# An adaLN block with sliding-window attention and a token-mixing MLP: V's outer rows copied from PSUM, two units' products moved ahead of their dense groups, the last quotients ahead of the last norm, the first group reordered

## The chip, the cores and the metric

One core of one Trainium2 chip runs the whole program. The metric is the device time of one execution in microseconds (us); the time before the change is the median of three runs. Engines are named as the profile names them: PE (TensorE matmuls), PEld (its weight loads), DVE (VectorE), ACT (ScalarE), POOL (GpSimd), SP (SyncE, which issues the DMAs here). Each engine works through its own instructions in order and waits on semaphores for the others.

## The reference, cut to what matters

```python
# x: 2048 x 512, 32 heads of 16, window of 256
h = _layernorm(x) * (1 + ca) + sa              # sa, ca, ga, sb, cb, gb = silu(c) @ w_mod
q, k, v = split(h @ wqkv)
p = softmax(where(0 <= i - j < 256, q @ k.T / 4, -1e9))
x = x + ga * ((p @ v) @ wo)
h = _layernorm(x) * (1 + cb) + sb
u = gelu(einsum('bsd,sf->bdf', _layernorm(h), w1) + b1)     # mixes the 2048 tokens, F = 1792
x = x + gb * transpose(einsum('bdf,fs->bds', u, w2) + b2)
```

## The kernel before

**Groups and units.** The 2048 tokens are worked in four groups `tg` of 512. In a group the 32 heads are taken eight at a time (`g8`), and eight heads make up to five units `k` (`KINDS`, L413): k = 0 and 1 are the inner keys of the even heads, k = 2 the outer rows of both parities (keys that share a 64-row half with their queries' block), k = 3 and 4 the inner keys of the odd heads. In the first group k = 0 and 3 are one unit for g8 > 0. This makes 77 units. Each has scores on PE (`emit_scores`), two exponentials of 128x1024 on ACT (`emit_exp`, L676) and products with V on PE (`av_a` L696 with `VaugT`, `av_c` L715 with `Vc`), which add up in the one PSUM bank `po`. V carries 16 columns of ones behind each head's 16 columns, so the row sums come out beside the products.

**PSUM.** The scores use three buffers of two banks (`pss`), the products one bank (`po`), and everything dense one bank (`dn`): a dense group must wait until DVE has evacuated the dense group before it.

**What else runs beside the attention.** One dense group is laid beside almost every unit by `plan` (L857): q, k and v projections of this group and the next (`qk_group`, `v_group`), the transposes of the normalised x, the output projection `wo_group`, and parts of the first MLP product (`part_group`, which need the blocks `hb`). Most dense groups are 16 matmuls and one evacuation on DVE.

**The order inside a unit u** (L1003 to L1061) is on PE: scores of unit u + 1, then the products of unit u - 1 if they close a sum (`closes`, L1026), then the dense group, then the products of unit u - 1 if they close nothing. The exponential of the first half is emitted ahead of all this and that of the second half behind the dense group.

**DVE and POOL** get the rest from `fill` (L818): a list of chains whose steps are taken when a hand-kept clock says that they fit before the next evacuation (`SLACK` 0.3 us plus `late[0]`). Chains are the statistics of the first norm, `norm_rest` (L753: reciprocal `zr` on DVE, the quotients `merge` on POOL at L760, a transpose `OTd` back on DVE at L768) and `ln23` (L771) for each of the first twelve token blocks: p1 statistics of the new x (DVE) and its reciprocal root (POOL, L208 and L212), p2 the norm on DVE (L788) and two passes over 128x512 on POOL (L792, L793), p3 statistics of the result (DVE) and `hb` on POOL (L219). p2 is free to start when fewer than `LIVE` = 4 blocks are under way.

**V's outer rows.** `v_group`'s evacuation (L303) copies PSUM to `VaugT` (L304), and for the third and fourth block of a group copies the first 64 rows of heads 0 to 7, values and ones, from there to `Vc` (L306). The other rows of `Vc` come by DMA (`copy_vc`).

**The start** (L547 to L577, L994 to L1035): the first group's q and k for the first eight heads come in pieces (`first_qk`), the four parts of the second k piece ahead of unit 0's scores; block 3 of V is computed at unit 1, behind the scores of unit 2.

**The end** (L1062 on): after the last products come `norm_rest` of the last eight heads, then `t_wo` (L1130), whose matmuls need `OTd`, among the first matmuls of the MLP's first product (L1111), the rest of it (L1197), and the second product (L1233).

Of the kernel before, what the change touches and what calls it, by code (L numbers as in the profile page):

```python
# [30 lines left out]
def kernel(  # L31
# [261 lines left out]
    def v_group(tg, tl, pool, name="dn"):  # L293
        def mms(parts=range(ND), pv=None):
            pv = pv or pool.tile([P, D], DT.float32, name=name)
            for dc in parts:
                dense(
                    pv, lhsT=h1T[tg][:, dc, tl * P : (tl + 1) * P],
                    rhs=wqkv[:, dc, 2 * D : 3 * D], start=(dc == 0), stop=(dc == ND - 1),
                )  # L300
            return pv

        def evac(pv):  # L303
            nc.vector.tensor_copy(out=VaugT[tg][:, tl, :, 0:DH], in_=pv[:].rearrange("p (h d) -> p h d", d=DH))  # L304
            if tl > 1:
                nc.vector.tensor_copy(out=Vc[0][0:64, tl, 0:8, :], in_=VaugT[tg][0:64, tl, 0:8, :])  # L306
        return mms, evac, 0.9 if tl > 1 else 0.7

    q_loads = []
# [59 lines left out]
    def bias_group(pool):  # L369
        def mms():  # L370
            pb = pool.tile([P, NF + NT], DT.bfloat16, name="dn")
            nc.tensor.transpose(pb[:], b12[:], identity[0 : NF + NT, 0 : NF + NT])
            return pb

        def evac(pb):
            nc.vector.tensor_copy(out=bFM[:], in_=pb[:])
        return mms, evac, 0.2
# [37 lines left out]
    with tc.manual_schedule():  # L415
# [98 lines left out]
        def ones(r):  # L514
            for b in range(4):
                nc.gpsimd.memset(Vring[r][:, b, :, DH : 2 * DH], 1.0)

        ones(0)

        def zeros_for(g8):  # L520
            for half in range(2):
# [51 lines left out]
            first_qk("k", dc, 0)  # L573
        q_half(0)
        k_piece(0)
        for dc in range(ND):
            first_qk("k", dc, 1)  # L577

        w1box = {}
# [191 lines left out]
        def ln23(tb):  # L771
            v = {}

            def stats(src, key):
                st = small.tile([P, nc.vector.BN_STATS_DIM], DT.float32, name="ln2_stats")
                nc.vector.bn_stats(out=st[:], in_=src)  # L776
                v[key] = small.tile([P, nc.vector.BN_AGGR_DIM], DT.float32, name="ln2_mv")
                nc.vector.bn_aggr(out=v[key][:], in_=st[:])  # L778
                v[key + "r"] = rstd_of(v[key][:, 1:2], 1, "ln2")

            def p1():
                stats(xres[tb][:], "m2")
                return 0.85

            def p2():
                live.add(tb)
                h2 = v["h2"] = lnpool.tile([P, D], DT.bfloat16, name="h2")
                nc.vector.tensor_scalar(  # L788
                    out=h2[:], in0=xres[tb][:], scalar1=v["m2"][:, 0:1], scalar2=v["m2r"][:],
                    op0=ALU.subtract, op1=ALU.mult,  # L790
                )
                nc.gpsimd.tensor_tensor(out=h2[:], in0=h2[:], in1=bc_cb1, op=ALU.mult)  # L792
                nc.gpsimd.tensor_tensor(out=h2[:], in0=h2[:], in1=bc_sb, op=ALU.add)  # L793
                return 2.4

            def p3():
                stats(v["h2"][:], "m3")
                apply_by_pool(hb[tb][:], v["h2"][:], v["m3"][:, 0:1], v["m3r"][:])
                done.add(tb)
                live.discard(tb)  # L800
                return 2.0
            return [(p1, 0.8), (p2, 0.37, lambda: len(live) < LIVE), (p3, 0.8)]

        chains = []
        live = set()
        loaded = set(range(8))
        clock = dict(pe=0.0, act=0.0, dve=0.0, pool=0.0, dn=0.0, po=0.0)

        held, late = [False], [0.0]

        def add_chain(steps, first=False):
            chains.insert(0 if first else len(chains), [list(steps), clock["dve"]])
# [44 lines left out]
        def plan(tg):  # L857
            at, then = {}, {}

            def lay(ul, group):  # L860
                assert ul not in at, (tg, ul)
                at[ul] = group

            def qk(ul, g, g8, kind):
                lay(ul, qk_group(g, g8, kind, ps_dn))

            if tg == 0:
                lay(0, v_group(tg, 1, ps_po, "po"))
                lay(2, qk_group(tg, 1, "k", ps_po, "po"))
                lay(3, v_group(tg, 2, ps_dn))  # L870
                for ul, g8, kind in ((1, 1, "q"), (4, 2, "q"), (5, 2, "k"), (6, 3, "q"), (7, 3, "k")):
                    qk(ul, tg, g8, kind)
                lay(8, bias_group(ps_dn))
                lay(9, bc_group(ps_dn))
                then[12] = [(lambda g=g: fold_wod(g), 0.0) for g in range(ND)]
            else:
                lay(0, v_group(tg, 2, ps_dn))
                lay(1, v_group(tg, 3, ps_dn))
                if tg == 1:
                    order = ((2, 1, "k"), (3, 2, "q"), (4, 2, "k"), (5, 3, "q"), (8, 3, "k"))  # L880
                else:
                    order = ((2, 2, "k"), (3, 3, "q"), (4, 3, "k"))
                for ul, g8, kind in order:
                    qk(ul, tg, g8, kind)
                for ul, fc, k in {2: ((8, 10, 0), (10, 11, 0)), 3: ((8, 13, 0), (10, 12, 0), (11, 12, 1))}.get(tg, ()):
                    lay(ul, part_group(fc, k))
                for ul in (6, 7, 9, 10) if tg == 1 else (5, 6, 7, 9):
                    tb = next(wo_next)
                    lay(ul, wo_group(tb, ps_dn))
                    then[ul] = ln23(tb)  # L890
            if tg + 1 < NG:
                t0, t1, q0, v0, k0, q1, v1 = (10, 11, 12, 14, 13, 16, 15) if tg == 0 else (11, 12, 13, 14, 15, 17, 16)
                lay(t0, transpose_group(tg + 1, 0, ps_dn))
                lay(t1, transpose_group(tg + 1, 1, ps_dn))
                lay(v0, v_group(tg + 1, 0, ps_dn))
                lay(v1, v_group(tg + 1, 1, ps_dn))
                for ul, g8, kind in ((q0, 0, "q"), (k0, 0, "k"), (q1, 1, "q")):
                    qk(ul, tg + 1, g8, kind)
                if tg:
                    qk(18, tg + 1, 1, "k")  # L900
                    qk(19, tg + 1, 2, "q")
            else:
                for n, fc in enumerate((6, 7, 8, 9)):
                    for k in range(2):
                        lay(12 + 2 * n + k, part_group(fc, k))
            return at, then
# [85 lines left out]
                on_pool(for_pool)  # L992

        emit_scores(0)  # L994
        for dc in range(ND):
            first_qk("q", dc, 1)
        q_half(1)
# [5 lines left out]
        for u, (tg, g8, k) in enumerate(units):  # L1003
# [19 lines left out]
                av_c(tg, g8, 1)  # L1023
            for n in range(3) if u == 4 else ():
                products(n)
            closes = u > 0 and units[u - 1][2] in (2, 4) and u != 3  # L1026
            if closes:
                products(u - 1)
            if u == 1:
                mms, evac, cost = v_group(0, 3, ps_s)  # L1030
                pv = mms(range(ND), ps_s.tile([P, 2, 4 * P], DT.float32, name="pss")[:, 0, :])
                clock["pe"] += 0.9
                evac(pv)
                ln1_stats(1, 1)
                clock["dve"] = max(clock["dve"], clock["pe"] + 0.05) + cost + 0.8  # L1035
            group = at.get(ul)
            held[0] = u < 4

            late[0] = 0.5 if 4 <= u < 8 else 0.12 if tg else 0.0
            if group:  # L1040
                tile_ = group[0]()
                clock["pe"] = max(clock["pe"], clock["dn"]) + (0.55 if group[2] > 1 else 0.2 if group[2] == 0.2 else 0.9)
# [2 lines left out]
            if group:  # L1045
                fill(clock["pe"] + 0.05)
                evacuate(group, tile_)
                if u == 1:
                    on_pool(1.0)
                    for tl in range(2):  # L1050
                        ln1_apply(1, tl)
                    on_pool(2.26)
                if ul in then:
                    add_chain(then[ul])
            if u > 3 and not closes:
                products(u - 1)
            if both(tg, g8, 0) and k == 4:
# [4 lines left out]
        u += 1  # L1062
        emit_av(u - 1)
        add_chain(norm_rest(NG - 1, ND - 1), first=True)
        while chains:
            clock["dve"] += 1.0
            fill(clock["dve"] + 9.0)
# [202 lines left out]
```

## Time and profile before

| what | value |
|---|---|
| three runs | 259.0, 257.82, 258.76 us; median 258.76 |
| the profiled execution's own time | 259.11 us |
| its span (first to last instruction) | 257.2 us |
| granted PE clock | 1.0 throughout |
| busy: PE, DVE, ACT, POOL | 239.2, 171.3, 159.3, 132.6 us |
| the exponentials (L676) | 154, busy 142.7 us, first at 12.8, last at 160.7 |
| the MLP's second product (L1233) | 238 matmuls, 48.5 us |

Times in views are counted from the span's start. A timeline row gives the start, the time that the merged instructions took, engine, line, operation, what it writes and reads, the count, and in brackets the idle time of the engine ahead of it with what ended it. A row "line engine op ... xcount | busy, mean ns | idle" groups all instructions of one line. A row of windows gives the busy time of each engine, with the count of its instructions, in one stretch of time.

### The profile page before, as it was taken

What the parts mean: (1) busy time and instruction counts of PE and PEld (TensorE: products, weight loads), DVE (VectorE), ACT (ScalarE), POOL (GpSimd) and SP (SyncE); (2) the same over time, 40 slices, a digit from 0 to 9 for tenths busy, and PEclk for the clock granted to TensorE, in tenths of its full rate; (3) what the DMA queues carried; (4) which work ended last, traced back from release to release, by engine and by line L of the source; (5) the groups of instructions that cost most, each with busy time, mean ns of one, the idle gap of its engine ahead of it and who ended that gap; (6) DMA issues with size and microseconds to landing.
All of it is one profiled execution on the core that took longest, in us unless ns stands there. A gap on an engine that the chain in (4) does not pass through costs nothing.

```text
span 257.2 us, 11303 instructions
## 1 busy us (share of the span) xinstructions
PE 239.2 (93%) x5011; PEld 127.3 (49%) x5011; DVE 171.3 (67%) x358; ACT 159.3 (62%) x187; POOL 132.6 (52%) x225
## 2 busy tenths in 40 slices
PE   7999889999899889999989999889999999999994
PEld 2644455555455455565555555444444444444443
DVE  5758789887887797887887888589603212332544
ACT  6388999999899899999999999100065220000000
POOL 5697876886468688568666499955300000000000
PEclk9999999999999999999999999999999999999999
DMA  5986715157422623201122200999930000202021
GB/s 176 324 260 199 218 59 144 36 144 195 130 66 70 171 49 66 56 4 34 31 60 57 55 3 14 331 414 409 412 144 0 0 0 3 82 0 82 33 92 41
DMA packets 26260, 29.96 MB, mean 116 GB/s; under 512 B 3940, under 2 KB 22884, under 8 KB 26212
## 3 DMA queue, kind: packets, MB, share of 16 engines
q1 hardware_dynamic: 26212, 29.25, 36.5%
q8 instruction: 39, 0.64, 1.0%
q14 instruction: 9, 0.07, 0.1%
HBM read 22.55 MB, written 2.23 MB: 96 GB/s over the span
## 4 chain that ended last, share of the span: by engine, by line
PE 62%; DVE 19%; POOL 12%; issue 3%; DMA 2%; SPq 1%; POOLq 0%
PE py L1233 19%; PE dn L288 14%; PE pu L1111 7%; PE pu L1197 6%; PE pss L609 4%; DVE t L748 3%; PE po L715 3%; PE po L696 3%; DVE VaugT L304 3%; POOL ln_rstd L212 2%; DMA wmod<-in_w_mod_dram 2%; POOL h L793 2%; POOL h L792 2%; DVE ln_stats L776 2%; POOL merge L760 2%
## 5 line engine op out<-in xcount | busy, mean ns | idle before, releaser
L676 ACT ACTIVATE et<-pss 128x1024 bf16<-128x1024 f32 (+1 forms) x154 | 142.7, 1025 | 6.5 <-PE pss L626 4.9
L1233 PE MATMUL py<-guT,w2r 128*128 128x512 bf16 (+1 forms) x238 | 48.5, 367 | 0.0
L1233 PEld LDWEIGHTS <-w2r 128*128 128x128 bf16 x238 | 23.3, 98 | 25.3
L288 PE MATMUL dn<-h1T,wqkv 128*32 128x512 bf16 (+1 forms) x480 | 31.4, 378 | 2.4 <-DVE VaugT L304 1.4
L1212 DVE SCALAR_TENSOR_TENSOR o<-py,bFM,bc 128x512 bf16<-128x512 f32 (+1 forms) x17 | 11.7, 714 | 30.5 <-PE py L1233 30.5
L748 DVE STREAM_TRANSPOSE t<-po 128x512 f32<-128x512 f32 x32 | 22.9, 714 | 6.9 <-PE po L715 4.3
L212 POOL TENSOR_TENSOR ln_rstd<-ln_ve,mhalf 128x1 f32<-128x1 f32 (+1 forms) x40 | 24.1, 603 | 3.4
L609 PE MATMUL pss<-QT,KT 32*128 32x64 bf16 (+2 forms) x704 | 25.4, 237 | 0.0
L696 PE MATMUL po<-et,VaugT 128*32 128x64 bf16 (+2 forms) x704 | 24.7, 240 | 0.7 <-DVE t L748 0.7
L696 PEld LDWEIGHTS <-VaugT 128*32 128x32 bf16 x704 | 18.1, 96 | 12.0 <-issue 4.2
L208 POOL TENSOR_SCALAR ln_ve<-ln_mv 128x1 f32<-128x1 f32 (+1 forms) x39 | 9.2, 235 | 24.6 <-DVE ln_mv L778 12.9
L609 PEld LDWEIGHTS <-KT 32*128 32x128 bf16 x704 | 13.9, 92 | 12.4 <-issue 3.8
L288 PEld LDWEIGHTS <-wqkv 128*32 128x32 bf16 x544 | 14.0, 95 | 11.7 <-issue 4.1
L792 POOL TENSOR_TENSOR h<-h,bc 128x512 bf16<-128x512 bf16 x12 | 13.9, 1161 | 8.7 <-DVE h L788 8.7
L1122 ACT ACT_TABLE_LOAD x1 | 1.3, 1283 | 27.0 <-issue 27.0
L760 POOL TENSOR_TENSOR merge<-t,zr 128x512 bf16<-128x512 f32 x16 | 17.0, 1060 | 0.9 <-DVE zr L759 0.9
L288 PE MATMUL dn<-wqkv,h1T 128*32 128x512 bf16 x224 | 15.0, 380 | 2.3 <-DVE VaugT L304 0.9
L626 PE MATMUL pss<-mask_q,mask_k 32*128 32x256 bf16 (+1 forms) x232 | 16.7, 266 | 0.0
L1120 DVE TENSOR_TENSOR gelu_a<-pu,part 128x512 f32<-128x512 f32 x8 | 5.2, 686 | 16.4 <-PE pu L1197 16.4
L288 PE MATMUL dn<-hb,w1a 128*32 128x512 bf16 x208 | 13.8, 380 | 0.9 <-DVE part L851 0.7
L793 POOL TENSOR_TENSOR h<-h,bc 128x512 bf16<-128x512 bf16 x12 | 13.9, 1158 | 0.9
L1197 PE MATMUL pu<-hb,w1b 128*128 128x512 bf16 x64 | 14.3, 379 | 0.0
(126 smaller groups left out, 376.9 us busy)
## 6 DMA issues: line engine op xcount, KB each, us to landing
w2r<-in_B_w_dram SPq DMA_DIRECT2D x14, 512.0 KB, 10.0
w1a<-in_B_w_dram SPq DMA_DIRECT2D x16, 224.0 KB, 3.6
w1b<-in_B_w_dram SPq DMA_DIRECT2D x8, 448.0 KB, 7.8
wmod<-in_w_mod_dram SPq DMA_DIRECT2D x8, 256.0 KB, 3.8
Vc<-VaugT SPq DMA_DIRECT2D x32, 64.0 KB, 2.4
out_dram<-otile SPq DMA_DIRECT2D x15, 128.0 KB, 1.7
x<-in_A_x_dram SPq DMA_DIRECT2D x7, 256.0 KB, 3.4
Vc<-VaugT SPq DMA_DIRECT2D x12, 128.0 KB, 3.4
```

The source lines that it names most:

```text
L212: nc.gpsimd.tensor_tensor(out=r[:], in0=ve[:], in1=mhalf[:, 0:n], op=ALU.pow)
L288: nc.tensor.matmul(out[cols, :], lhsT=lhsT[:, cols], rhs=rhs, start=start, stop=stop, tile_position=(0, 32 * j), skip_group_check=True,)
L609: nc.tensor.matmul(pss[j // 2][:, j % 2, c0 : c0 + nq], lhsT=keys(kb, g8)[rows[j], k0 : k0 + P], rhs=QT[tg][g8][rows[j], p, q0 : q0 + nq], ...
L676: act = nc.scalar.activation(out=et[:, :, 0:n], in_=state.pop((u, a))[:, :, 0:n], func=ACT.Exp, scale=SCORE_SCALE,)
L696: nc.tensor.matmul(state["po"][32 * j : 32 * j + 32, q0 : q0 + nq], lhsT=VaugT[kb // 4][:, kb % 4, 8 * g8 + 2 * j + par, :], rhs=state["e" ...
L748: nc.vector.transpose(out=state["t2"][:, par, :], in_=state["po"][:])
L760: nc.gpsimd.tensor_tensor(out=m[:].rearrange("p (b a d) -> p a b d", a=2, d=DH), in0=t2v[:, :, :, 0:DH], in1=zr[:].to_broadcast([P, 2, 16, ...
L792: nc.gpsimd.tensor_tensor(out=h2[:], in0=h2[:], in1=bc_cb1, op=ALU.mult)
L793: nc.gpsimd.tensor_tensor(out=h2[:], in0=h2[:], in1=bc_sb, op=ALU.add)
L1111: nc.tensor.matmul(pu[:, i, :], lhsT=w1_of(sc, fc), rhs=hb[sc][:], start=(sc == 0), stop=(sc == NT - 1),)
L1197: nc.tensor.matmul(pu[:, i, :], lhsT=w1_of(sc, fc), rhs=hb[sc][:], start=(sc == s0), stop=(sc == NT - 1),)
L1233: nc.tensor.matmul(pys[n][:, 0 : hi - lo], lhsT=w2r[:, fc, tb * P : (tb + 1) * P], rhs=guT[fc][:, lo:hi], start=(fc == 0), stop=(fc == NF ...
```

## The change

It has four parts.

1. **V's outer rows.** The copy into `Vc` reads the PSUM tile instead of `VaugT` and takes the 16 value columns of each head, not the ones; the ones are set once, by a memset on POOL at the start.
2. **Products.** From the second token group on `closes` is true for every k but 4, so the products of k = 0 and k = 1, which stood behind the dense groups of the units k = 1 and k = 2, stand ahead of them.
3. **The end.** In the last three units no step p2 may start (`ending`); it may again behind the last `norm_rest`.
4. **The first group.** Two of the four parts of the second k piece stand behind unit 0's scores; block 3 of V is computed at unit 0, behind its dense group, ahead of the scores of unit 2; `bc_group` and `bias_group` change places; `late[0]` is 0.5 for units 4 and 5 only, and 0.16 instead of 0.12 from the second group on.

The changed program's order, engine by engine, differs as follows. ACT's is the same. PE and DVE have the same count of instructions, POOL one more (the memset). On DVE one step of a chain changes places with an evacuation here and there from the second half of the first group on. On POOL the last `merge` stood behind p2 of block 11 and ahead of its p3; it now stands behind both, and the p1, p2 and p3 steps of blocks 7 to 11 stand earlier among the merges and evacuations by one to four steps.

```diff
@@ v_group @@
             if tl > 1:
-                nc.vector.tensor_copy(out=Vc[0][0:64, tl, 0:8, :], in_=VaugT[tg][0:64, tl, 0:8, :])
+                nc.vector.tensor_copy(
+                    out=Vc[0][0:64, tl, 0:8, 0:DH], in_=pv[0:64, 0 : 8 * DH].rearrange("p (h d) -> p h d", d=DH),
+                )
...
         ones(0)
+        nc.gpsimd.memset(Vc[0][0:64, 2:4, 0:8, DH : 2 * DH], 1.0)
...
-        for dc in range(ND):
+        for dc in range(2):
             first_qk("k", dc, 1)
...
-            return [(p1, 0.8), (p2, 0.37, lambda: len(live) < LIVE), (p3, 0.8)]
+            return [(p1, 0.8), (p2, 0.37, lambda: len(live) < LIVE and not ending[0]), (p3, 0.8)]
...
-                lay(8, bias_group(ps_dn))
-                lay(9, bc_group(ps_dn))
+                lay(8, bc_group(ps_dn))
+                lay(9, bias_group(ps_dn))
...
         emit_scores(0)
+        for dc in range(2, ND):
+            first_qk("k", dc, 1)
         for dc in range(ND):
             first_qk("q", dc, 1)
...
-            closes = u > 0 and units[u - 1][2] in (2, 4) and u != 3
+            closes = k != 4 if tg else u > 0 and units[u - 1][2] in (2, 4) and u != 3
             if closes:
                 products(u - 1)
-            if u == 1:
-                mms, evac, cost = v_group(0, 3, ps_s)
...
-                clock["dve"] = max(clock["dve"], clock["pe"] + 0.05) + cost + 0.8
             group = at.get(ul)
             held[0] = u < 4
-            late[0] = 0.5 if 4 <= u < 8 else 0.12 if tg else 0.0
+            ending[0] = u >= len(units) - 3
+            late[0] = 0.5 if 4 <= u < 6 else 0.16 if tg else 0.0
             if group:
...
                 if ul in then:
                     add_chain(then[ul])
+            if u == 0:
+                mms, evac, cost = v_group(0, 3, ps_s)
...
+                clock["dve"] = max(clock["dve"], clock["pe"] + 0.05) + cost + 0.8
             if u > 3 and not closes:
                 products(u - 1)
...
         add_chain(norm_rest(NG - 1, ND - 1), first=True)
+        ending[0] = False
         while chains:
```

More of the change, by code (lines that the diff above doesn't have):

```diff
@@ L807 @@
         clock = dict(pe=0.0, act=0.0, dve=0.0, pool=0.0, dn=0.0, po=0.0)
-        held, late = [False], [0.0]
+        held, late, ending = [False], [0.0], [False]
         def add_chain(steps, first=False):
@@ L1025 @@
                 products(n)
-            closes = u > 0 and units[u - 1][2] in (2, 4) and u != 3
+            closes = k != 4 if tg else u > 0 and units[u - 1][2] in (2, 4) and u != 3
             if closes:
                 products(u - 1)
-            if u == 1:
-                mms, evac, cost = v_group(0, 3, ps_s)
[L1031 to L1034, printed above, removed]
-                clock["dve"] = max(clock["dve"], clock["pe"] + 0.05) + cost + 0.8
             group = at.get(ul)
             held[0] = u < 4
-            late[0] = 0.5 if 4 <= u < 8 else 0.12 if tg else 0.0
+            ending[0] = u >= len(units) - 3
+            late[0] = 0.5 if 4 <= u < 6 else 0.16 if tg else 0.0
             if group:
@@ L1054 @@
                     add_chain(then[ul])
+            if u == 0:
+                mms, evac, cost = v_group(0, 3, ps_s)
+                pv = mms(range(ND), ps_s.tile([P, 2, 4 * P], DT.float32, name="pss")[:, 0, :])
+                clock["pe"] += 0.9
+                evac(pv)
+                ln1_stats(1, 1)
+                clock["dve"] = max(clock["dve"], clock["pe"] + 0.05) + cost + 0.8
             if u > 3 and not closes:
```

## The prediction

> **What bounds the kernel now.** I read the windows first (busy time of each engine by stretch), then ACT's rows of the timeline, then the timeline around each gap.
>
> ```profile
> span 257.2 us, 11303 instructions
> ...
> 31.50:52.20 20.70, 18.40 (x625) 10.90 (x613) 18.03 (x37) 20.66 (x22) 16.04 (x21) 1.00 0.30 81
> ...
> 161.80:168.00 6.20, 4.47 (x52) 2.15 (x45) 3.26 (x6) 0.00 (x0) 5.66 (x9) 1.00 0.96 340
> 168.00:257.20 89.20, 85.79 (x411) 40.00 (x410) 37.70 (x78) 10.09 (x15) 8.19 (x19) 1.00 0.31 120
> ```
>
> The columns are PE, PEld, DVE, ACT, POOL. In the attention ACT hardly rests: from 31.5 us it is busy 20.66 of 20.70 us. From 168 us PE is busy 85.8 of 89.2 us (the rest is the last evacuation and store), so whatever lets it enter that stretch earlier comes off the end. Between them, at 161.8 to 168, PE is busy 4.47 of 6.20 us and POOL 5.66. The attention can therefore gain only by closing gaps between exponentials:
>
> ```profile
> 19.57 1.09 ACT L676 ACTIVATE et<-pss 128x512 bf16<-128x512 f32 x2 [1.02 <-PE pss L626]
> ...
> 25.34 1.94 ACT L676 ACTIVATE et<-pss 128x1024 bf16<-128x1024 f32 x2 [0.50 <-PE pss L626]
> ...
> 27.54 3.81 ACT L676 ACTIVATE et<-pss 128x1024 bf16<-128x1024 f32 x4 [0.26 <-PE pss L656]
> 31.51 20.67 ACT L676 ACTIVATE et<-pss 128x1024 bf16<-128x1024 f32 x22 [0.16 <-PE pss L616]
> 52.51 15.00 ACT L676 ACTIVATE et<-pss 128x1024 bf16<-128x1024 f32 x16 [0.34 <-PE pss L626]
> 68.22 20.43 ACT L676 ACTIVATE et<-pss 128x1024 bf16<-128x1024 f32 x22 [0.71 <-PE pss L626]
> 89.45 3.92 ACT L676 ACTIVATE et<-pss 128x1024 bf16<-128x1024 f32 x4 [0.79 <-PE pss L656]
> 93.88 37.71 ACT L676 ACTIVATE et<-pss 128x1024 bf16<-128x1024 f32 x40 [0.52 <-PE pss L626]
> 132.01 29.76 ACT L676 ACTIVATE et<-pss 128x1024 bf16<-128x1024 f32 x32 [0.42 <-PE pss L626]
> ```
>
> The brackets are what there is to win: 1.94 us up to 31.5 in the rows shown and 2.78 after it. An exponential takes 29.76/32 = 0.93 us, so a unit takes 1.86.
>
> **The start (part 4).**
>
> ```profile
> 11.54 0.96 PE L288 MATMUL po<-h1T,wqkv 128*32 128x384 bf16 x16
> ...
> 16.96 0.24 PE L646 MATMUL pss<-QT,KT 32*64 32x128 bf16 x2 [0.59 <-issue]
> ...
> 22.73 0.66 DVE L306 COPY Vc<-VaugT 64x256 bf16<-64x256 bf16 x1
> ...
> 23.45 0.24 PE L715 MATMUL po<-et,Vc 128*32 128x64 bf16 x8 [0.31 <-DVE Vc L306]
> ```
>
> Half of the 16 matmuls at 11.54, some 0.45 us, goes behind unit 0's scores, and unit 1's slip by about 0.4: a loss that must be won back. It is: PE then stands still for 0.59 us ("issue") in unit 2's scores, and V's block 3 (16 matmuls like those at 50.71 below, 1.05 us) now lies ahead of them instead of behind. It covers the standstill: the scores start at about 17.1, where they resumed at 16.96 before, and the next ones come some 0.6 earlier. The exponentials at 19.57 are then held by the pair before them, itself late, which I see end at 19.3: **0.25 gained**. At 23.45 PE waits for V's copy of 0.66 us; a copy of 0.26 (next part) brings the products, and the DVE work queued behind them, **0.4** forward. The gap of **0.16** at 31.5 follows a q evacuation that now stands ahead of the transpose it waited behind. Sum **-0.8**, between +0.4 (nothing won back) and -1.94 (all these gaps).
>
> At nothing I put the memset (POOL waits for DVE's statistics behind it; uncovered, less than the 1.15 us of a full pass at 164.93), `late`, and `bc_group` one unit earlier: ACT has no gap there, and its store and four loads wait in SP's queue ahead of the output projection's weights, which POOL folds four units later. Were they late, POOL would hold up the next group's normalised x.
>
> **V's copies and the products (parts 1 and 2).**
>
> ```profile
> L306 DVE COPY Vc<-VaugT x8: 220/598/1026, 19.2 to 130.2; 64x256 bf16<-64x256 bf16 x8
> ...
> L376 DVE CAST bFM<-dn 128x30 f32<-128x30 bf16 x1 | 0.1, 149 | 0.0
> ...
> 50.71 1.05 PE L288 MATMUL dn<-wqkv,h1T 128*32 128x512 bf16 x16 [0.41 <-DVE VaugT L304]
> 51.80 0.69 DVE L304 CAST VaugT<-dn 128x512 bf16<-128x512 f32 x1
> ...
> 92.08 1.05 PE L288 MATMUL dn<-h1T,wqkv 128*32 128x512 bf16 x16 [0.74 <-DVE VaugT L304]
> ...
> 127.17 0.63 DVE L304 CAST VaugT<-dn 128x512 bf16<-128x512 f32 x1
> 127.83 0.93 DVE L306 COPY Vc<-VaugT 64x256 bf16<-64x256 bf16 x1
> ...
> 129.49 0.66 DVE L304 CAST VaugT<-dn 128x512 bf16<-128x512 f32 x1
> 130.20 1.05 PE L288 MATMUL dn<-h1T,wqkv 128*32 128x512 bf16 x16 [0.65 <-DVE VaugT L304]
> 131.06 0.41 PE L696 MATMUL po<-et,VaugT 128*32 128x256 bf16 x12
> 131.41 0.40 PE L609 MATMUL pss<-QT,KT 32*128 32x256 bf16 x12
> ```
>
> The old copy takes 0.22 to 1.03 us. No row has the new one, 128 values from PSUM. It lies between 30 values (0.15) and 512 (0.69 at 51.80); on the line between them, 1.12 ns each, it is **0.26**. I take that, nearest the small row, with 0.15 and 0.69 as ends. [...]
>
> The price is elsewhere: the copy is a second reader of `dn`. From a dense group to its evacuation is 1.09 us (50.71 to 51.80), from there to the next group 0.71 (129.49 to 130.20): 1.80 a unit. With 0.26 more a V unit takes 2.06 against ACT's 1.86. Against that, the products (0.35 us of PE, 131.06 to 131.41) now run while PE waits for `dn`. Third group of V pairs, before the gap at 132.0: evacuation 127.17, copy done 128.06, dense group 128.1, its evacuation 129.19 to 129.87, copy to 130.13, next dense group 130.18 (was 130.20), scores 0.35 earlier: **-0.35** of the 0.42. Before 93.9 the same walk starts the dense group of 92.08 some 0.12 earlier, with the products **-0.47** of 0.52. Before 52.5 the old copy was near its minimum and the second reader costs twice 0.26, less 0.35: **+0.17**. Sum **-0.65**. A copy of 0.69 would cost 0.43 more in six V units, 2.6 us; one of 0.15 gains 0.6.
>
> In the other units the products only change places with a dense group inside PE's wait for ACT: nothing. The products that open `po` wait for DVE's transpose of it; a dense group and 40 score matmuls still lie between the two, and only if DVE came to that transpose over 1 us late would PE, and the dense group behind, stand.
>
> **The end (part 3).**
>
> ```profile
> 137.04 0.63 DVE L397 TENSOR_TENSOR x<-dn,x 128x512 bf16<-128x512 f32 x1
> ...
> 144.13 0.22 POOL L208 TENSOR_SCALAR ln_ve<-ln_mv 128x1 f32<-128x1 f32 x1 [3.45 <-DVE ln_mv L778]
> ...
> 163.69 1.16 POOL L792 TENSOR_TENSOR h<-h,bc 128x512 bf16<-128x512 bf16 x1
> 163.77 0.35 DVE L759 RECIPROCAL zr<-t 128x32 f32<-128x32 f32 x1
> 164.93 1.15 POOL L793 TENSOR_TENSOR h<-h,bc 128x512 bf16<-128x512 bf16 x1
> 166.04 1.06 POOL L760 TENSOR_TENSOR merge<-t,zr 128x512 bf16<-128x512 f32 x1
> 167.13 0.71 DVE L768 STREAM_TRANSPOSE OTd<-merge 128x512 bf16<-128x512 bf16 x1
> ...
> 167.18 0.22 POOL L208 TENSOR_SCALAR ln_ve<-ln_mv 128x1 f32<-128x1 f32 x1
> ...
> 167.90 1.25 PE L1133 MATMUL pa<-wod,OTd 128*128 128x512 bf16 x5 [1.73 <-DVE OTd L768]
> ...
> 168.52 0.77 POOL L219 TENSOR_SCALAR hb<-h,ln_rstd,shift 128x512 bf16<-128x512 bf16 x1
> ```
>
> `zr` is ready at 164.12, but POOL is in p2's two passes of the last block until 166.08; then come `merge`, `OTd`, and PE, which stood 1.73 us. In the changed order these passes stand two merges earlier, but the last block's p3 comes ahead of `merge` too. That pays only if POOL, without rest since 144.1, starts sooner. It idled 3.45 us there, and p1 of block 8 now follows its x (137.04) directly: POOL can start at about 138.7. From there to the last `merge` the new order has four p1, four p2, four p3 and three merges. By the rows a p2 is 2.4 us (163.69 to 166.04), a p3 2.1 (167.18 to 169.29), a p1 that without shift and `hb`, some 1.0, a merge 1.06: 9.6 + 8.4 + 4.0 + 3.2 = 25.2, so 163.9 with no wait. `merge` can't end before 164.12 + 1.06 = 165.2. I add 0.4, because block 11's statistics on DVE stand behind two transposes of the units that ACT paces: `merge` ends at 165.6, `OTd` at 166.3, PE goes on at 166.35. **-1.55**, between 0 and -1.73.
>
> **Sum:** -0.8 - 0.65 - 1.55 = -3.0. The profiled execution took 259.11 us (span 257.2 and 1.9 around it), so 256.1; it stands 0.35 above the median of 258.76, on which the forecast is **255.8**.
>
> **Rivals.**
>
> 1. *The V units win nothing*: the second reader eats what the products free, and the start's 0.4 is not won back in full. Only the end and 0.3 remain: 256.9. For it: 2.06 against 1.86. Against: the walk at 130.2.
> 2. *The last quotients still wait*: POOL is 1.5 us later than walked, p3 ends at 166.0 and `merge` starts where it did. 257.3. For it: p3's 2.1 us newly ahead. Against: the idle 3.45.
> 3. *Slower: DVE's filler goes ahead of evacuations.* The clock counts the moved products 0.34, PE takes about 0.2 beyond its overlap, and `late` gives 0.04 more, so `fill` may put a step (0.7 to 0.9 us) ahead of a dense evacuation. Scores have some 0.35 us before ACT starves, so each such place costs about 0.5; nothing below a delay of 0.35. At nine of the 24 units touched it is 4.5 us: 260.3. For it: in the changed order `OTd` stands ahead of the evacuation of block 9's x. Against: there it is late by 0.3 only.
> 4. *PE's "issue" stops go.* 0.71 and 0.79 of the gaps follow PE standing for 0.73 and 0.63 us with nothing to wait for:
>
> ```profile
> 66.39 0.21 PE L715 MATMUL po<-et,Vc 128*32 128x64 bf16 x3 [0.73 <-issue]
> ...
> 88.01 0.83 PE L288 MATMUL dn<-wqkv,h1T 128*32 128x512 bf16 x11 [0.63 <-issue]
> ```
>
> I keep them. If they are accidents of what DMA ran beside them and fall elsewhere, 1.5 us goes: 254.3. [...]
>
> **How the numbers follow.** Forecast 0.50; rivals 1 to 4: 0.16, 0.12, 0.13, 0.09. 0.5% (1.3 us), about what a measurement here can tell, puts the bounds at 257.5 and 260.1. Each case has its own spread. Faster: 0.45 of the forecast's 0.50, 0.10 of the first, 0.05 of the second, 0.08 of the fourth: 0.68. Slower: 0.11 of the third, 0.03 of the second with a PSUM copy near its far end: 0.14. Same: the other 0.18. The range reaches to the fourth rival and, above, to the copy's far end with part of the third: 254.2 to 259.6; outside it some 0.2.
>
> **What would show it.** Right: no gap near 19; the copies at 0.26 beside a busy POOL; gaps under 0.2 at 94 and 132; the last `merge` within 0.5 us of `zr` and PE's wait for `OTd` under 0.4. Wrong: a copy over 0.4, PE waiting longer for `dn` at V's blocks, the exponentials ending after 160.3, POOL still in p3 when `zr` is done plus a microsecond.

## The result, and the profile after

| | before | after |
|---|---|---|
| median of the runs of one comparison (22 each) | 258.87 us (257.82 to 259.68) | 257.34 us (256.88 to 259.46) |
| the profiled execution | 259.11 us, span 257.2 | 257.06 us, span 255.2 |

The ratio of after to before is 0.9952, with a 95% interval of 0.9936 to 0.9968: 1.2 us faster, between 0.8 and 1.7; the two medians lie 1.5 apart. I had forecast 255.8, three microseconds less than before. The two profiled executions differ by 2.05 us, as that of before lay above its median and that of after below.

The first view is the page's head and ACT's rows of the timeline after, to be held against those of before: start, time taken, count of exponentials, and in brackets the pause ahead of them with what ended it.

```profile
span 255.2 us, 11295 instructions
...
17.21 8.84 ACT L680 ACTIVATE et<-pss 128x1024 bf16<-128x1024 f32 x10 [0.84 <-PE pss L660]
26.31 24.65 ACT L680 ACTIVATE et<-pss 128x1024 bf16<-128x1024 f32 x26 [0.26 <-PE pss L660]
51.40 11.54 ACT L680 ACTIVATE et<-pss 128x1024 bf16<-128x1024 f32 x12 [0.44 <-PE pss L630]
63.24 31.98 ACT L680 ACTIVATE et<-pss 128x1024 bf16<-128x1024 f32 x34 [0.30 <-PE pss L630]
95.51 7.44 ACT L680 ACTIVATE et<-pss 128x1024 bf16<-128x1024 f32 x8 [0.29 <-PE pss L630]
104.14 5.83 ACT L680 ACTIVATE et<-pss 128x1024 bf16<-128x1024 f32 x6 [1.20 <-PE pss L630]
110.21 15.19 ACT L680 ACTIVATE et<-pss 128x1024 bf16<-128x1024 f32 x16 [0.24 <-PE pss L630]
125.62 35.91 ACT L680 ACTIVATE et<-pss 128x1024 bf16<-128x1024 f32 x38 [0.23 <-PE pss L630]
```

The pauses that were to go are gone: no row starts near 19, 93.9 or 132.0. Others have come: 0.84 us at 17.21, 1.20 at 104.14, and some of 0.2 to 0.3 where there were none.

A list of pauses does not say where time was won and lost. For that I compare the same exponential in both kernels (both have 154), read from narrow windows of the same view. First before, then after; the starts of the 19th and the 83rd exponential of before, 31.51 and 93.88, are in the prediction's rows.

```profile
105.28 1.94 ACT L676 ACTIVATE et<-pss 128x1024 bf16<-128x1024 f32 x2
159.82 1.95 ACT L676 ACTIVATE et<-pss 128x1024 bf16<-128x1024 f32 x2
```

```profile
30.38 1.94 ACT L680 ACTIVATE et<-pss 128x1024 bf16<-128x1024 f32 x2
91.44 1.94 ACT L680 ACTIVATE et<-pss 128x1024 bf16<-128x1024 f32 x2
104.14 1.94 ACT L680 ACTIVATE et<-pss 128x1024 bf16<-128x1024 f32 x2 [1.20 <-PE pss L630]
159.53 2.00 ACT L680 ACTIVATE et<-pss 128x1024 bf16<-128x1024 f32 x2
```

These rows begin with the 19th, 83rd, 95th and 153rd exponential (the two of before with the last two). After is ahead by 31.51 - 30.38 = 1.13 us at the 19th, by 2.44 at the 83rd, by 1.14 at the 95th and by 0.29 at the 153rd; this distance is called the lead below. More than two microseconds were won and lost again inside the attention. Over half of the loss came at one place, POOL's and PE's rows of the timeline after:

```profile
93.14 1.16 POOL L796 TENSOR_TENSOR h<-h,bc 128x512 bf16<-128x512 bf16 x1 [0.23 <-DVE h L792]
...
101.18 0.83 PE L288 MATMUL dn<-hb,w1a 128*32 128x512 bf16 x12
...
102.39 0.77 POOL L219 TENSOR_SCALAR hb<-h,ln_rstd,shift 128x512 bf16<-128x512 bf16 x1
...
103.21 0.40 PE L288 MATMUL dn<-hb,w1a 128*32 128x512 bf16 x4 [1.20 <-POOL hb L219]
```

POOL has no rest from 93.14 until `hb` of block 3 is written at 103.16: in these 10.02 us it is busy 8.98, with no pause over 0.11 between two instructions. Twelve matmuls of the dense group are done by 102.0; the last four need that block, and PE stands 1.20 us.

The copies of V's outer rows and the end after (seven of the eight copies read `dn` and stand in this row; the eighth, at the start, took 0.27 too):

```profile
L307 DVE CAST Vc<-dn x7: 266/273/273, 21.8 to 129.5; 64x128 bf16<-64x128 f32 x7
```

```profile
163.21 0.35 DVE L763 RECIPROCAL zr<-t 128x32 f32<-128x32 f32 x1
163.29 0.77 POOL L219 TENSOR_SCALAR hb<-h,ln_rstd,shift 128x512 bf16<-128x512 bf16 x1
164.02 1.06 POOL L764 TENSOR_TENSOR merge<-t,zr 128x512 bf16<-128x512 f32 x1
...
165.12 0.71 DVE L772 STREAM_TRANSPOSE OTd<-merge 128x512 bf16<-128x512 bf16 x1 [1.56 <-POOL merge L764]
165.88 1.25 PE L1142 MATMUL pa<-wod,OTd 128*128 128x512 bf16 x5 [0.28 <-DVE OTd L772]
```

A copy takes 0.27 us (shortest, median and longest in ns). `merge` follows `zr` by 0.46 us, and PE's wait for `OTd` is 0.28 instead of 1.73.

### The profile page after: what moved, and what is told of

The parts are those of the page before. It is cut to its first block, busy times and chain, and to the rows that moved or that the text cites. A ratio compares the mean times of both kernels' runs of the same rounds, so it can differ in the third digit from the quotient of the medians.

```text
span 255.2 us, 11295 instructions
## 1 busy us (share of the span) xinstructions
PE 242.3 (95%) x5002; PEld 123.3 (48%) x5011; DVE 169.7 (66%) x358; ACT 159.5 (62%) x187; POOL 133.0 (52%) x226
## 4 chain that ended last, share of the span: by engine, by line
PE 68%; DVE 12%; POOL 8%; DMA 3%; ACT 3%; issue 3%; SPq 2%; DVEq 0%; POOLq 0%; ACTq 0%
PE py L1242 19%; PE dn L288 17%; PE pu L1120 7%; PE pu L1206 6%; PE pss L613 5%; PE po L700 3%; PE po L719 3%; ACT et L680 2%; DMA wmod<-in_w_mod_dram 2%; DVE t L752 2%; PE pss L630 2%; POOL merge L764 2%; SPq L317 1%; DVE OTd L772 1%; PE pss L650 1%
## 5 line engine op out<-in xcount | busy, mean ns | idle before, releaser
L1221 DVE SCALAR_TENSOR_TENSOR o<-py,bFM,bc 128x512 bf16<-128x512 f32 (+1 forms) x17 | 11.6, 714 | 30.5 <-PE py L1242 30.5
L700 PE MATMUL po<-et,VaugT 128*32 128x64 bf16 (+2 forms) x704 | 25.3, 242 | 0.6 <-DVE t L752 0.2
L700 PEld LDWEIGHTS <-VaugT 128*32 128x32 bf16 x704 | 15.7, 95 | 13.5 <-issue 8.8
```

Source lines behind the costliest of these rows:

```text
L700: nc.tensor.matmul(state["po"][32 * j : 32 * j + 32, q0 : q0 + nq], lhsT=VaugT[kb // 4][:, kb % 4, 8 * g8 + 2 * j + par, :], rhs=state["e" ...
```

## The experiments

All were compared with the kernel before on the same chip. The table cuts each profiled execution at the same exponentials: start of the span to the 19th, from there to the 95th (this holds the wait for `hb` of block 3), to the 153rd, and from the end of the last exponential to the end of the span. The ratio is from the timed runs.

| run | ratio to before, 95% interval | to 19th | 19th to 95th | 95th to 153rd | behind the last |
|---|---|---|---|---|---|
| before | 1 | 31.5 | 73.8 | 54.5 | 95.5 |
| e8 before, again | | 31.5 | 74.7 | 54.8 | 95.3 |
| after | 0.9952 (0.9936 to 0.9968) | 30.4 | 73.8 | 55.4 | 93.7 |
| e3 end alone | 0.9971 (0.9949 to 0.9994) | 31.5 | 73.6 | 54.5 | 94.7 |
| e5 products alone | 0.9934 (0.9908 to 0.9960) | 32.1 | 73.1 | 55.3 | 93.7 |
| e4 without start | 0.9929 (0.9900 to 0.9958) | 30.8 | 72.7 | 55.3 | 93.7 |
| e6 copy from SBUF | 0.9966 (0.9943 to 0.9989) | 30.4 | 73.8 | 55.7 | 93.7 |
| e2 products back | 1.0009 (0.9985 to 1.0033) | 30.4 | 75.6 | 56.1 | 93.7 |
| e1 part later | 0.9925 (0.9895 to 0.9956) | 30.6 | 72.4 | 55.5 | 93.7 |
| e10 before, part later | 0.9951 (0.9929 to 0.9973) | 32.1 | 73.7 | 54.4 | 95.4 |
| e9 bias first | 0.9901 (0.9873 to 0.9928) | 30.5 | 73.7 | 55.3 | 93.7 |
| e11 late 0.17 | 0.9915 (0.9885 to 0.9945) | 30.7 | 73.6 | 55.1 | 93.7 |
| e7 late 0.20 | 1.0107 (1.0069 to 1.0145) | 30.4 | 75.9 | 56.9 | 93.9 |
| e12 steps behind | 0.9903 (0.9873 to 0.9934) | 30.7 | 72.8 | 55.1 | 93.7 |

One profile is one execution: the second of before, e8, is 1.0 us longer than the first in its span. So the columns tell where, and the ratios how much. Two entries of 32.1 are not of their edits, as e5 and e10 have the first group of before: in e5 PE stood 1.30 us at 17 us with nothing to wait for, and in e10 the first exponential came at 14.01 instead of 12.81. The profiled execution of e10, 259.38 us, is also the longest of its ten.

**e1_part_later.** After, with two dense groups of the third token group exchanged, so that PE asks for `hb` of block 3 one unit later:

```diff
-                for ul, fc, k in {2: ((8, 10, 0), (10, 11, 0)), ...
+                for ul, fc, k in {2: ((9, 10, 0), (10, 11, 0)), ...
-                for ul in (6, 7, 9, 10) if tg == 1 else (5, 6, 7, 9):
+                for ul in ((6, 7, 9, 10), (5, 6, 7, 8), (5, 6, 7, 9))[tg - 1]:
```

> The kernel after, with one edit: in the third token group the dense group of unit 8 (first MLP product, needs the blocks hb 0 to 3) and that of unit 9 (output projection) change places, so that PE asks for hb of block 3 one unit (1.86 us) later. In the profile after, PE waited 1.20 us there, and the lead of the exponentials over those of before fell from 2.31 to 1.13 us. Theory 1 (that one wait took the gain, and nothing behind it asks for it again): the wait is gone or under 0.2, the lead at exponential 95 stays at 2.0 to 2.3, and the kernel is about 1.0 us faster than after: 256.3, or 2.5 us under before. Rival (DVE and POOL set the pace there; what is won at this wait is lost again at the next due block): the wait is gone but the lead is back at 1.1 or less by exponential 117, and the time is that of after within 0.4: 257.0 to 257.4.

The wait is gone. The group that asks for `hb` runs through, after a short wait for an evacuation:

```profile
103.47 1.05 PE L288 MATMUL dn<-hb,w1a 128*32 128x512 bf16 x16 [0.18 <-DVE x L400]
```

The lead at the 95th is 105.28 - 103.04 = 2.24, as theory 1 had it, and 256.66 us is nearer to its time than to the rival's. The interval overlaps that of after, so the time alone would not settle it. Behind the 95th both kernels lose the same (55.5 and 55.4 us for a stretch of 54.5).

**e10_before_part_later.** The same edit on the kernel before.

> The kernel before with the same edit as the run with the part later: in the third group the dense group that needs hb of blocks 0 to 3 stands at unit 9 instead of 8. Theory 1 (the wait for hb of block 3 was the limit of before already: 1.0 us in its second profile, 0.19 only where an issue stop had held PE up ahead of it): 0.4 to 0.9 us under before, 258.2 to 258.6. Rival (the wait is born with the change): before's time within 0.2.

0.9951, 1.3 us faster with an interval of 0.7 to 1.8, more than theory 1 gave and as much as the whole change: the limit was there before. Its profile has no wait for `hb`. A second profile of before shows how the wait hid.

**e8_before_again.**

> The kernel before once more, for a second profile of it. Theory 1 (PE's issue stops of 0.73 at 66.4 and 0.63 at 88.0 belong to this program's layout and come in each execution): both are there again, within 0.2 us. Rival (they are accidents of an execution): one or both are gone or elsewhere, and where the one at 88 is gone, PE waits for hb of block 3 by about 1.0 us and the exponentials end within 0.3 us of where they did.

```profile
67.53 0.21 PE L715 MATMUL po<-et,Vc 128*32 128x64 bf16 x3 [1.26 <-issue]
...
105.29 0.40 PE L288 MATMUL dn<-hb,w1a 128*32 128x512 bf16 x4 [1.01 <-POOL hb L219]
```

Each theory is half right. The stop at 66 is there again, and longer; that at 88 is absent, and PE waits 1.01 us for `hb` in its place. In the first profile the stop had used up the slack, and the wait showed as 0.19. The run e3 below, which has the same order up to there, also has no stop at 88 and a wait of 1.0 for `hb`. Beside e8, with a stop like its own at 66, e10 takes 1.0 us less from the 19th to the 95th (73.7 and 74.7). Three more programs with the old order of products have the stop at 66 (0.8 in e3, 1.4 in e2, 1.4 in e10); after and the others with the new order have no stop above 0.3 there, though e5 and e7 have one of 0.5 at 70 to 71. That at 88 came in no second profile (e7 stops for 0.24 at 89).

**e3_end_alone.** Before, with part 3 alone (the four lines of `ending`).

> The kernel before with part 3 alone: no step p2 starts in the last three units. Theory (the end's gain is its own, 1.78 us from the last exponential to PE's wait for OTd in the traces): 1.5 to 1.8 us under before, 257.1 to 257.4, PE's wait for OTd falls from 1.73 to about 0.3, and the exponentials end where they did. If that is so, the other three parts together brought nothing to the time of after. Rival (the end's gain needs the attention's lead, as POOL must start early): 0.5 us or less under before, 258.4, with POOL in p3 of block 11 when zr is done.

0.75 us, half of what theory gave. The interval, 0.2 to 1.3, holds the rival's time too, but not its reason: `merge` does not wait for p3. DVE's, PE's and POOL's rows show why:

```profile
164.73 1.15 POOL L792 TENSOR_TENSOR h<-h,bc 128x512 bf16<-128x512 bf16 x1
...
167.13 0.69 DVE L776 BATCH_NORM_STATS2 ln_stats<-h 128x6 f32<-128x512 bf16 x1 [1.63 <-POOL h L793]
...
168.67 1.02 PE L1135 MATMUL pa<-wod,OTd 128*128 128x512 bf16 x4 [0.56 <-DVE x L1139]
...
170.19 1.02 PE L1135 MATMUL pa<-wod,OTd 128*128 128x512 bf16 x4 [0.50 <-DVE x L1139]
```

`merge` is early, but p2 of the last block had not been begun when the guard closed, so all of it came behind. Its statistics then stood on DVE ahead of the evacuations of `pa`, and PE waited 0.56 + 0.50 us for these. Beside the new order of products the guard (`ending`) changes nothing: e4, which has it, and e5, which has not, run the same steps of DVE and POOL in the same order, the memset apart.

**e5_products_alone.** Before, with `closes` as in part 2 and late 0.16.

> The kernel before with part 2 alone: products of k = 0 and 1 ahead of the dense groups from the second token group on, and late 0.16 instead of 0.12. Its order on POOL is that of the run without the start: hb of block 3 ahead of the third group's normalised x, and p1, p2 and p3 of block 11 ahead of the last merge, although no guard on p2 is in it. Theory 1 (the products and the places that the planner gives to the steps of the later norms because of them bring nearly all, the end included; the copy and the start add little): 257.2 to 257.8, no wait of PE for hb of block 3, PE's wait for OTd at 0.3. Rival (as I predicted, the end is the worth of the guard, and the products bring 0.3 to 0.6 by themselves): 258.3 to 258.8, with PE's wait for OTd at 1.7.

1.7 us faster, as theory 1 had it, and no less than the whole change (the intervals overlap): after, which has the other three parts too, is no faster. PE's wait for `OTd` fell without the guard:

```profile
166.75 1.25 PE L1133 MATMUL pa<-wod,OTd 128*128 128x512 bf16 x5 [0.26 <-DVE OTd L768]
```

**e4_without_start.** After, with the first group as before (part 4 undone except late 0.16).

> The kernel after with the first group put back as it was before (four parts of the second k piece ahead of unit 0's scores, block 3 of V at unit 1, bias ahead of bc, late 0.5 for units 4 to 7; 0.16 later stays). Theory (the start's lead of 1.13 us at exponential 19 is real and reaches the end unless a wait behind takes it): the lead at exponential 19 is 0 to 0.4, and if the wait for hb of block 3 shrinks by what the lead shrinks, the time is that of after, 257.3 to 257.6. Rival (the start's gain is carried through): 1.1 us slower than after, 258.4.

Neither: 257.07 us, not slower than after. The start is 0.4 us longer (30.8), but there is no wait for `hb`: `hb` of block 3 comes on POOL ahead of three of the third group's four normalised x, and 19th to 95th is 1.1 us shorter. This put the suspicion on the order that the hand-kept clock makes.

**e9_bias_first.** After, with one edit:

```diff
-                lay(8, bc_group(ps_dn))
-                lay(9, bias_group(ps_dn))
+                lay(8, bias_group(ps_dn))
+                lay(9, bc_group(ps_dn))
```

> The kernel after with one edit: bias_group stands ahead of bc_group again, as before. Nothing of it is near the stretch in question, but the hand-kept clock then comes to the third group a little differently, and hb of block 3 stands on POOL ahead of the third group's normalised x, as in the run without the start. Theory 1 (the start, the copy and the products each win what I gave them or more, and after lost about 1 us of it where PE waits for hb of block 3, because of a place in POOL's order): no wait for hb, lead at exponential 95 of 2.0 or more, and 1.0 us faster than after: 256.1 to 256.6, the fastest run so far. Rival (the lead can't be kept, since DVE's later steps, put ahead of evacuations, take it back whatever the order): 257.0 or more, with the lead under 0.6 at the last exponential.

0.9901 and 256.68 us: 1.3 us faster than after, with intervals that don't touch. The profiled execution, at 256.99 above the median, doesn't show this gain (its span is 255.1, that of after 255.2). It shows the wait gone: POOL writes the block eight microseconds ahead of PE's use (the first two rows).

```profile
93.77 0.77 POOL L219 TENSOR_SCALAR hb<-h,ln_rstd,shift 128x512 bf16<-128x512 bf16 x1
...
102.56 1.05 PE L288 MATMUL dn<-hb,w1a 128*32 128x512 bf16 x16
...
122.27 0.85 DVE L792 TENSOR_SCALAR h<-x,ln_mv,ln_rstd 128x512 bf16<-128x512 bf16 x1
...
123.03 0.67 DVE L333 CAST KT<-dn 128x512 bf16<-128x512 f32 x1
...
123.76 1.05 PE L288 MATMUL dn<-h1T,wqkv 128*32 128x512 bf16 x16 [0.38 <-DVE KT L333]
...
125.56 1.94 ACT L680 ACTIVATE et<-pss 128x1024 bf16<-128x1024 f32 x2 [0.49 <-PE pss L630]
```

The lead at the 95th was expected at 2.0 and is 1.13: this execution paused for 0.38 at 47.8 and 0.29 at 88.5, where after did not. The last four rows show how such a loss comes about. A step of the later norms, `h`, is taken ahead of the evacuation of `KT`; PE's next dense group waits 0.38 for the bank, the scores behind it are late, and ACT pauses 0.49.

Against e4 this run also tests the start: but for one step each, DVE and POOL have the same order in both. It is 0.7 us faster by ratio, with overlapping intervals.

**e11_late_017** and **e7_block3_earlier.** After, with late 0.17 or 0.20 for 0.16.

> The kernel after with late at 0.17 from the second group on, half way on the planner's scale to none of the steps but enough to change places: hb of block 3 stands ahead of two of the third group's normalised x. Theory 1 (what decides is the order that falls out, and not late by itself; this order has no wait for hb, and few steps ahead of evacuations): no wait for hb, 256.2 to 257.0. Rival (a larger late costs in itself, as the run at 0.20 was 4 us slower than after): 257.8 or more, with PE's waits for q's evacuations over 1.5 us in sum.

> The kernel after with late at 0.20 instead of 0.16 from the second token group on and nothing else. The planner then takes the steps of blocks 1 to 3 one place earlier, and hb of block 3 stands on POOL ahead of three of the four normalised x. Theory 1 (after lost its lead at the wait for hb of block 3; with the start's lead kept and no such wait, the exponentials come out further ahead than in any run so far): lead at exponential 95 of 2.2 or more, 256.2 to 256.6. Rival (each step that is put ahead of an evacuation costs about 0.3 of lead, and 0.20 puts more of them there): no wait for hb, but the lead falls elsewhere, 257.3 or more.

0.17 gives 256.68 us, as theory 1 had it; 0.20 gives 261.73, where it failed and the rival was too mild. In neither does PE wait for `hb`. At 0.20, in the list of PE's waits and in the timeline:

```profile
PE dn L288 <- DVE qs L336: 2.5, 5, 0.8
```

```profile
81.18 1.14 DVE L792 TENSOR_SCALAR h<-x,ln_mv,ln_rstd 128x512 bf16<-128x512 bf16 x1 [0.15 <-POOL ln_rstd L212]
...
82.24 0.68 DVE L304 CAST VaugT<-dn 128x512 bf16<-128x512 f32 x1
...
82.97 1.05 PE L288 MATMUL dn<-h1T,wqkv 128*32 128x512 bf16 x16 [1.10 <-DVE VaugT L304]
...
84.55 1.02 ACT L680 ACTIVATE et<-pss 128x1024 bf16<-128x1024 f32 x1 [0.93 <-PE pss L630]
```

Behind q's evacuations PE waits 2.5 us in five places (0.5 in two in after). The chain of e9 comes again, larger: `h`, 1.14 us long, stands ahead of V's evacuation, PE is 1.10 late and ACT pauses 0.93.

**e12_steps_behind.** e9 with late 0.12 for units 47 to 57, which puts some of these steps behind evacuations.

> The kernel of the run with bias first, with late at 0.12 for units 47 to 57 only (0.16 before and after). POOL's order of merges, norms and hb stays as in that run, but on DVE the norm h of two blocks, two transposes OTd and a statistics step that stood ahead of an evacuation there stand behind it. In that run's profile the h ahead of k's evacuation at 122.3 took 0.85 us beside a pass of POOL, PE then waited 0.38 for KT, and the exponentials paused for 0.49 at 125.6; another 0.28 at 106.4. Theory (a step ahead of an evacuation costs lead, as the slow run at late 0.20 shows): the pauses at exponentials 97 and 117 are under 0.15, and the kernel is 0.3 to 0.8 us faster than the run with bias first: 255.9 to 256.4. Rival (what is put back makes a later step late, so the work only moves): the two pauses go and others come, within 0.2 us of that run: 256.5 to 256.9.

The pause at 125.6 is gone: `h` stands behind the evacuation, and PE waits for nothing worth a note.

```profile
122.14 0.69 DVE L333 CAST KT<-dn 128x512 bf16<-128x512 f32 x1 [0.17 <-PE dn L288]
...
122.88 1.05 PE L288 MATMUL dn<-h1T,wqkv 128*32 128x512 bf16 x16
...
124.62 0.41 DVE L792 TENSOR_SCALAR h<-x,ln_mv,ln_rstd 128x512 bf16<-128x512 bf16 x1
```

The other of the two stayed, at 0.27, and 0.19 came at 113.3. The ratio is that of e9, as the rival had it; the median, 256.23, is in the theory's range, but before was quicker beside it too, and the intervals could hide some tenths. e9 and e12 beat both kernels, by 2.5 us against before.

**e2_products_back.** After, with the products of k = 0 and 1 emitted behind the dense groups, the clock counting them as after does (part 0 counts, 1 emits).

```diff
+        def products(u, part=2):
...
-                products(u - 1)
+                products(u - 1, 2 if units[u - 1][2] in (2, 4) else 0)
...
+            if closes and units[u - 1][2] in (0, 1):
+                products(u - 1, 1)
```

> The kernel after, with the products of k = 0 and k = 1 of the later token groups emitted behind the dense groups again, as before, while the hand-kept clock goes on counting them where after does, so that DVE's and POOL's orders stay those of after. Theory 1 (the moved products help at V's blocks and cost nothing elsewhere, as predicted): the gaps of ACT at the V pairs come back, 0.35 us a pair in three pairs, so about 0.6 to 1.0 us slower than after, 258.1. Rival (in the other units the products stand between the scores and the dense group, and delay dense group, evacuation and next scores by 0.1 to 0.2 in each unit k = 1, which I read from gaps of 0.12 at exponentials 47, 57, 107, 127 and 137): those gaps go, the V pairs cost, and the sum is between -0.6 and 0, 256.8 to 257.3.

1.5 us slower than after, more than theory 1 gave, and the rival fell, though the pauses of 0.12 at the 47th, 127th and 137th exponential did go. PE's waits name the price of a second reader of `dn` that nothing fills:

```profile
PE dn L288 <- DVE Vc L307: 2.5, 6, 0.7
```

Part of the loss is the stop at 66 (1.4 us here).

**e6_copy_from_sbuf.** After, with the old copy.

> The kernel after with the old copy: V's outer rows, values and ones, copied from VaugT in SBUF. All orders are those of after. Theory 1 (the copy from PSUM is worth what the walk gave: 0.4 at the start, and about 0.3 in a V pair whose old copy lies beside POOL's passes, less the second reader's 0.26 a unit where it doesn't; what is won ahead of the wait for hb of block 3 is lost there): 0.2 to 0.6 slower than after, 257.5 to 257.9. Rival (the second reader of dn costs more than the copy's stretching): 0.3 or more faster, 257.0.

257.93 us, where theory 1 ends, but by ratio 0.4 us slower than after with overlapping intervals: the copy's worth is not settled by time. Nor is it by e4 and e5, which have DVE's and POOL's steps in one order and the new and the old copy: 0.9929 and 0.9934.

## Why the prediction was wrong, step by step

**The start, -0.8: right in size in the trace, wrong as a sum.** The lead at the 19th is 1.13 us. I added 0.4 for the copy to the rest. But the start with the old copy (e6) has 1.09 there, and the copy without the start (e4) has 0.70, with 0.45 of it won between the 9th and 13th exponential, where the copy is. By these profiles, one of each run, the two do not add. After begins its first exponential 0.45 earlier than the first profile of before, but that is not the reason: e8 and e3 begin 0.3 earlier and come to the 19th at 31.5 all the same. In time the start is not settled (e9 against e4).

**V's copies and pairs, -0.65: right in size.** The copy takes 0.27 (0.26 given), where the old one took 0.22 to 1.03. The lead grows by 0.42 at the pair of 93.9 (0.47 given) and by 0.32 at that of 132 (0.35), and falls by 0.2 to 0.3 at that of 52.5 (0.17). At 93.9 it is the products: with the old copy the lead grows there by 0.49 (e6) and 0.53 (e5). At 132 the old copy gives 0.23 in e5 and a loss of 0.09 in e6.

**The end, -1.55: right in size, wrong in cause.** From the last exponential's end to PE's going on with `OTd` it was 6.13 us and is 4.35: 1.78. I gave that to part 3. It comes with the products and late 0.16 (e5), which put the last block's steps early enough; the guard by itself wins half and costs the rest in a new wait (e3).

**"At nothing I put ... `late`, and `bc_group` one unit earlier": this step failed.** I priced these edits by the work that stands beside them and looked for a gap of ACT there. Their effect lies far behind, through the clock: `bc_group` stands at 30 us and PE's wait for `hb` at 103. Exchanging `bc_group` and `bias_group` back makes the kernel 1.3 us faster (e9). Without that one edit the change is worth 2.6 us, between 1.9 and 3.3, and my 3.0 lies inside. For `late`, 0.04 more makes the kernel 4.0 us slower (e7 against after, by ratio); what 0.16 instead of 0.12 is worth by itself no run shows.

**The sum, -3.0, added wins that don't add.** In the profiled pair the end won its 1.78, but the attention only 0.24 of 1.45: the exponentials end at 161.53, not by 160.3. From the 19th to the 95th exponential the profiled after takes 73.8 us, as before, though the stretch to the 83rd is 1.3 us shorter: what is won there, two stops of PE included that I had left in, PE gives back waiting for `hb` of block 3. That this limit holds is shown by e1 (2.24 of lead kept), by e10 (before gains 1.3 by asking for it later) and by the runs side by side. Of those with the products in their new place, after and e6 wait for the block and are at 0.9952 and 0.9966; e1, e4, e5, e9, e11 and e12 don't, and are at 0.9901 to 0.9934. Only e7 has no such wait and is slower, by its waits for evacuations. The trace of before had the wait already, of 0.19 us, with a POOL that took no rest over 0.11 us in the eight microseconds ahead of it; I passed over it as small:

```profile
94.27 1.15 POOL L792 TENSOR_TENSOR h<-h,bc 128x512 bf16<-128x512 bf16 x1 [0.30 <-DVE h L788]
...
103.52 0.77 POOL L219 TENSOR_SCALAR hb<-h,ln_rstd,shift 128x512 bf16<-128x512 bf16 x1
...
104.34 0.40 PE L288 MATMUL dn<-hb,w1a 128*32 128x512 bf16 x4 [0.19 <-POOL hb L219]
```

From the 95th on I gave -0.35, and the stretch became 0.8 longer; by the trace this is the largest miss, 1.2 us. It is 0.6 to 2.4 longer in every run with late 0.16 or more, and that holds for e2 too (1.6), where PE has the products in their old place and DVE and POOL the order of after. So it goes with the order of the steps more than with the products' place. There the steps ahead of evacuations cost; e7 and e9 show the mechanism, but how much of the 0.8 it is stays open, since e12 took one such pause away and won only 0.2 of it in the trace and nothing in time.

**The rivals.** The third, DVE's filler ahead of evacuations, is real: at the two places shown PE waited 0.38 and 1.10 us and ACT paused 0.49 and 0.93, and at 0.20 it decides (1.07% slower than before). The fourth was half right: the stop at 66 goes with the order of the products, if not always without another a little later (e5, e7), and the one at 88 came in one execution alone. But the 1.5 us did not reach the end, for the wait for `hb` took as much. The first and second did not happen as told.

**"In the other units the products only change places: nothing": right.** The exponentials of units k = 1 come about 0.17 later and those of k = 3 are back by as much in most groups of heads.

## What to carry to other kernels

A short wait for an engine that never rests is a due date without slack: before wins along a stretch are added up, look for the next such place, and cap the sum there. Where a hand-kept clock decides the order, no edit in front of it can be put at nothing; compare each engine's order, and price every step that changed places with an evacuation. And one profile can carry a microsecond of chance (before and e8 span 257.2 and 258.2 us), so a small wait that stands right behind a stop should be read as about the stop's length plus its own: 0.19 behind the stop of 0.63 in before, 1.01 without that stop in e8. Ask also where the profiled execution lies among the timed ones: those of e9 and e10 did not show what their medians did.

## What was not expected of the hardware

Two of PE's issue stops come back at their place in the program, but not with their length: 0.59, 0.95 and 0.89 us at 17 in before, e8 and e3, and 0.73, 1.26, 0.81, 1.4 and 1.4 at 66 to 68 in before, e8, e3, e2 and e10. At 17 us PE goes on at 16.96 in before and at 16.98 in e8, and the earlier it comes there, the longer it stands. The trace of before shows what its three stops go with. The profile has a DMA queue of kind "instruction", `q8`, with 39 transfers of 16 KB in before and in after, one in about 4 us of the attention. In before three of them end at 15.52, 65.12 and 86.60 us, and PE goes on at 16.96, 66.39 and 88.01, 1.3 to 1.5 us later; the last of them took 2.24 us where the median is 0.96. Of the 19 other waits of PE of 0.25 us or more that before and after have in the attention, one ends so near behind a transfer (1.50, at 92.08 in before). That PE waits there for its own next instructions is my reading of the queue's kind and of these times; it was not shown, as no run moved a transfer. Most of the 39 cost nothing: the 14 traces have 13 stops of 0.4 us or more, and none has over three.

In e6 an old copy beside POOL's memsets took nearly ten times its shortest, 0.22:

```profile
16.01 1.94 POOL L523 MEMSET Vc<- 64x1024 bf16 x2
...
17.31 2.12 DVE L306 COPY Vc<-VaugT 64x256 bf16<-64x256 bf16 x1
```

and `h`, some 0.4 us alone, took 0.6 to 1.24 where it met a pass of POOL for most of its time (after, e7, e9), while all eight copies out of PSUM in after stayed at 0.27, four of them beside such a pass for their whole length. What makes the difference the rows do not show.
